# One more output row reads the last frequency pair in place, and two table quarters are transposed earlier

## The chip, the cores and the metric

The kernel runs on one core of one Trainium2 chip. The metric is the device time of one execution in microseconds; the time given for a kernel is the median of its runs. A profile is of one execution, and its own time is named beside it.

## What is computed

A long-convolution block with a token-mixing MLP behind it, on 2048 tokens of 448 channels:

```python
def _A_ref(q, k, v, shift_k, ssm_k, ssm_D):
    k_shift = sum of 4 shifted copies of k, each times a column of shift_k
    kv = k_shift * v
    y = irfft(rfft(kv padded to 4096) * rfft(ssm_k padded to 4096))[:2048]
    y = y + kv * ssm_D
    return q * y
def _B_ref(x, w1, b1, w2, b2):
    h = _layernorm(x)                       # over the channels
    u = gelu(einsum("bsd,sf->bdf", h, w1) + b1)
    return transposed(einsum("bdf,fs->bds", u, w2) + b2)
x = A_q
h = x + _A_ref(_layernorm(x), A_k, A_v, A_shift_k, A_ssm_k, A_ssm_D)
h2 = h + _B_ref(_layernorm(h), B_w1, B_b1, B_w2, B_b2)
```

S is 2048, D is 448, F is 1792; inputs and output are bfloat16.

## The kernel before

**Tiling.** A token index is split as 16 q + r: 128 partitions q and R = 16 rows r. All of SBUF is one tensor, `arena`, all of PSUM one tensor, `ps` (eight banks), so the profile names only these two; its line numbers tell the steps apart. The steps have tags, which are also the names in the order lists.

**Stages.** The transform of length 4096 is done as matmuls in two steps each way. `kT` and `kv` transpose the filter and form kv. `k1` and `u1` (`emit_stage1`, L1059) are the first forward step for the filter and for kv; the result goes by DMA from one layout to the next (L1075). `k2` and `u2` (`emit_stage2`, L1094) are the second forward step, in place in TK and TU; the evictions are those of `evac` (L738 and L739 on ScalarE, L741 and L742 on VectorE). `i1` (`emit_products_i1`) works by eight pairs: two products on VectorE (L1160), 16 matmuls (L1177), two evictions (halves h = 0 and 1) back into TU, and then DMAs that carry the pair from TU to TZ, where a partition holds one frequency (L1200, L1189). The pairs run in the order 0, 6, 3, 4, 5, 2, 1, 7: i1.1, i1.14, i1.8, i1.10, i1.12, i1.6, i1.4 and i1.16 are the names of their matmul steps, so i1.4 is pair 1 and i1.16 is pair 7, the last. `i2` (`emit_i2`) is the second inverse step, row by row: two matmuls (L1299) of ET, the transposed sine table, with TZ.

**In-place rows.** For rows r < NZ, here rows 0 and 1, TZ holds zeros in the place of the last pair, and four more matmuls (L1307) add that pair from TU directly, with EW as the table. EW is filled by POOL (zeros, L1134) and by small DMAs of parts of ET (L1127). These rows need not wait for the last pair's DMA; rows from NZ on do. The four stand behind the two TZ matmuls of their row.

**Behind i2.** A gate (L1316 on ScalarE, L1318 on VectorE; rows 0 to 3 have none, their normalised input XN comes from `xn`, L1269), a combination with the input on VectorE (L1326, L1337), then the second and third layernorm: rows 0 and 1 one at a time (L1343, L1346, L1375), the others by groups of two with a square on ScalarE (L1355), small steps on POOL (L1365 to L1375) and a power on POOL (L1379). A normalised row Q is written by VectorE (L1385). `mlp` accumulates over the rows: mlp.r is seven matmuls with Q row r (L1432); then come the other half of the first layer (L1442) and the second layer (L1453, with the last addition at L1456).

**Sine table.** `ct` makes ET from E by 8 transposes (L1108) and one eviction a quarter. Quarter 0 (step ct0.0) is made within i1, quarters 1 to 3 (steps ct.0, ct.1, ct.2) behind pair 7's matmuls, among warm-up matmuls (`warm`, L1210) that keep PE at work while it waits.

**Order.** A planner in the kernel puts every operation on an engine and finds the semaphores, but each engine's sequence is written out in `ORDER`, in one list each for pe, act, dve, pool and sp. An engine works its list strictly in order; a token such as `i1.16:18` is operation 18 of that step. The parts around the change are:

```python
"pe":  ... u1.15:0-7 k2.2:0-3 ... i1.16:1-7 i1.16:10-16 ... ct.2:0-7 warm.12:0 warm.3:0 ct.0:0-7 ct.1:0-6 warm.2:0 i2.1:0-1 i2.2:0-3 ...
"act": ... i1.4:8 i1.4:17 xn.1:0 xn.2:0 i1.16:18 i1.16:9 ct.2:8 ct.0:8 xn.5:0 xn.4:0 ct.1:8 i2.29:0 ...
"dve": ... u1.11:8 k2.3:4 k2.7:4 bias.1:0 k2.11:4 k2.15:5 u2.1:5 ... i1.9:0 ct0.0:8 q.1:0 ...
"sp":  ... ct0.1:5 ct0.1:2-4 i1.1:20 ... i1.4:20 i1.16:22 i1.16:20 i1.16:19 w1a.1:0 ...
```

`bias.1` is the cast of b2 (L939). `q` holds the statistics of the input rows (VectorE L1236, L1238; POOL L1244, L1247). The W1 loads from w1a.1 on wait for the four DMAs of pair 7.

## Time and profile before

| | us |
|---|---|
| median of the three runs | 173.62 |
| lowest and highest run | 172.66, 175.37 |
| the profiled execution | 172.93 |
| its span | 171.0 |

| engine | busy us | share of the span |
|---|---|---|
| PE (matmul) | 162.0 | 95% |
| PEld (weight load) | 95.1 | 56% |
| DVE (VectorE) | 98.9 | 58% |
| ACT (ScalarE) | 92.9 | 54% |
| POOL (GpSimd) | 60.3 | 35% |

In the profile, times are in microseconds from the start of the span. A timeline row gives start, length, engine, line, operation, what is written and read, the count, and in brackets the idle time ahead of it with what ended it. A row of the chain gives start, length and what the chain stood on. Instructions of one engine overlap a little at their ends, so a row's length is somewhat more than the time to the next start. The granted clock of PE is 1.00 in the whole span.

### The profile page before, as it was taken

The numbers are of one execution on the slowest core, as the hardware profiler recorded it, in microseconds if no ns is written. First come the engines' busy times: TensorE is split into PE (matmuls) and PEld (weight loads), VectorE is DVE, ScalarE is ACT, GpSimd is POOL, SyncE is SP. The second block draws the span as 40 slices with busy tenths as digits, with TensorE's granted clock in tenths as the row PEclk, the third lists the DMA queues.
The fourth block names the chain that finished last, engine by engine and source line by source line (L and its number), as shares of the span: only waits on it lengthen the run. The fifth ranks groups of instructions, "written<-read, shape, count | busy, mean of one in ns | idle before, by whom it ended". The sixth has DMA issues, their size and how long they took to land.

```text
span 171.0 us, 3568 instructions
## 1 busy us (share of the span) xinstructions
PE 162.0 (95%) x1425; PEld 95.1 (56%) x1425; DVE 98.9 (58%) x187; ACT 92.9 (54%) x133; POOL 60.3 (35%) x154
## 2 busy tenths in 40 slices
PE   6989999988889999999999999999999999999993
PEld 2766745442334443464455555555567777777783
DVE  7988988869699999999968810000003223132232
ACT  3698787998889999999887437321210000000000
POOL 8346627591810496576888820000000000000000
PEclk9999999999999999999999999999999999999999
DMA  5999677675859667665999999970000111101111
GB/s 167 406 310 384 192 246 274 246 281 210 270 147 372 236 182 217 186 185 183 319 361 404 413 419 421 418 324 13 0 0 4 54 54 54 54 0 58 54 54 54
DMA packets 15740, 35.15 MB, mean 206 GB/s; under 512 B 3628, under 2 KB 9980, under 8 KB 15724
## 3 DMA queue, kind: packets, MB, share of 16 engines
q1 hardware_dynamic: 12924, 29.08, 47.2%
q0 software_dynamic: 2656, 5.76, 10.5%
q8 instruction: 11, 0.18, 0.4%
q10 hardware_dynamic: 144, 0.08, 0.2%
q14 instruction: 5, 0.04, 0.1%
HBM read 22.05 MB, written 1.84 MB: 140 GB/s over the span
## 4 chain that ended last, share of the span: by engine, by line
PE 66%; ACT 14%; DMA 12%; DVE 3%; issue 2%; SPq 2%; POOL 0%; DVEq 0%
PE ps L1453 25%; PE ps L1442 12%; PE ps L1432 11%; ACT arena L738 7%; DMA arena<-arena 7%; DMA arena<-in_A_ssm_k_dram 5%; PE ps L1094 5%; ACT arena L1069 4%; PE ps L1177 4%; PE ps L1059 2%; PE ps L1299 2%; ACT arena L1316 2%; PE ps L992 1%; DVE arena L742 1%; PE ps L1307 1%
## 5 line engine op out<-in xcount | busy, mean ns | idle before, releaser
L1456 DVE SCALAR_TENSOR_TENSOR arena<-ps,arena 128x448 bf16<-128x448 f32 (+2 forms) x17 | 11.2, 656 | 57.4 <-PE ps L1453 57.3
L1453 PE MATMUL ps<-arena 128*128 128x448 bf16 (+2 forms) x238 | 42.7, 342 | 0.0
L1453 PEld LDWEIGHTS ps<-arena 128*128 128x128 bf16 x238 | 33.3, 145 | 9.5
L738 ACT CAST arena<-ps 128x896 bf16<-128x896 f32 x30 | 24.6, 1021 | 0.5 <-PE ps L1094 0.5
L1432 PE MATMUL ps<-arena 128*128 128x448 bf16 x112 | 22.5, 353 | 0.0
L1069 ACT CAST arena<-ps 128x896 bf16<-128x896 f32 x24 | 20.5, 915 | 3.7 <-PE ps L1059 3.7
L1075 POOL DMA_DIRECT2D arena<-arena x32 | 17.6, 553 | 12.7 <-ACT arena L1069 11.1
L1442 PE MATMUL ps<-arena 128*128 128x448 bf16 x112 | 21.3, 352 | 0.0
L1422 ACT ACTIVATE arena<-ps,arena 128x448 bf16<-128x448 f32 x14 | 8.2, 639 | 18.7 <-PE ps L1442 14.6
L1094 PE MATMUL ps<-arena 128*64 128x448 bf16 x128 | 15.2, 359 | 2.9 <-ACT arena L1069 0.9
L1160 DVE TENSOR_TENSOR arena<-arena 128x1792 bf16<-128x1792 bf16 x16 | 16.7, 1086 | 0.3 <-ACT arena L738 0.3
L1432 PEld LDWEIGHTS ps<-arena 128*128 128x128 bf16 x112 | 10.8, 98 | 10.6 <-DVE arena L1385 0.9
L1442 PEld LDWEIGHTS ps<-arena 128*128 128x128 bf16 x112 | 11.0, 98 | 10.2
L1059 PE MATMUL ps<-arena 128*32 128x448 bf16 x256 | 15.0, 355 | 0.8 <-DVE arena L1007 0.5
L1177 PE MATMUL ps<-arena 64*128 64x448 bf16 x128 | 14.5, 351 | 0.1
L1200 POOL DMA_DIRECT2D arena<-arena x15 | 8.7, 583 | 13.8 <-ACT arena L738 13.8
L1094 PEld LDWEIGHTS ps<-arena 128*64 128x64 f16 x128 | 6.2, 108 | 10.8 <-ACT arena L738 3.0
L1177 PEld LDWEIGHTS ps<-arena 64*128 64x128 f16 x128 | 6.1, 94 | 8.2 <-ACT arena L738 2.5
L1007 DVE TENSOR_TENSOR arena<-ps,arena 128x512 bf16<-128x512 f32 (+1 forms) x16 | 9.1, 618 | 2.1 <-PE ps L992 1.8
L1355 ACT ACTIVATE arena<-arena 128x448 bf16<-128x448 bf16 x14 | 8.0, 572 | 3.7 <-DVE arena L1326 3.6
L738 ACT COPY arena<-ps 128x1024 bf16<-128x1024 bf16 (+1 forms) x8 | 8.1, 1073 | 3.3 <-PE ps L966 3.3
L1059 PEld LDWEIGHTS ps<-arena 128*32 128x32 f16 x256 | 5.1, 95 | 7.6 <-DVE arena L1007 2.5
(97 smaller groups left out, 194.4 us busy)
## 6 DMA issues: line engine op xcount, KB each, us to landing
arena<-in_B_w_dram SPq DMA_DIRECT2D x8, 896.0 KB, 9.5
arena<-in_B_w_dram SPq DMA_DIRECT2D x2, 2048.0 KB, 17.8
arena<-arena POOLq DMA_DIRECT2D x32, 112.0 KB, 3.1
arena<-arena SPq DMA_DIRECT2D x16, 224.0 KB, 3.3
arena<-in_B_w_dram SPq DMA_DIRECT2D x2, 1536.0 KB, 20.3
arena<-in_A_k_dram SPq DMA_DIRECT2D x4, 448.0 KB, 6.0
arena<-in_A_v_dram SPq DMA_DIRECT2D x4, 448.0 KB, 9.0
arena<-in_A_q_dram SPq DMA_DIRECT2D x4, 448.0 KB, 5.5
```

The costliest lines, as they stand in the source:

```text
L738: return e.copy(out=dst(), in_=src())
L1007: return e.tensor_tensor(out=v, in0=u.rearrange("p t (r d) -> p t r d", d=64), in1=v, op=ALU.mult)
L1059: op("pe", lambda e, W, b=b, r=r, q=q, x=x, c0=c0: e.matmul(PS[32 * q:32 * q + 32, b.slots[x], 0:D], E[:, 2 * r + x, c0:c0 + 32], src[:, r ...
L1069: return e.copy(out=dst, in_=Ppair(b)) if W == "act" else e.tensor_copy(out=dst, in_=Ppair(b))
L1075: shuf[tag].append(op(q_, lambda e, W, g=g, i=i, a=a, nu=nu, jh=jh: e.dma_start(T[a + i:a + i + 4 * nu - 3:4].rearrange("p (j k) c d -> p ...
L1094: op("pe", lambda e, W, b=bs[h], h=h, j=j, c=c, par=par: e.matmul(PS[64 * par:64 * par + 64, b.slots[c], 0:D], FW[:, 64 * c:64 * c + 64], ...
L1160: op("dve", lambda e, W, m=m, i=i: e.tensor_tensor(out=MR(m.slots[0]).rearrange("p (x y) d -> p x y d", x=2), in0=TU[:, i].unsqueeze(2).br ...
L1177: k = op("pe", lambda e, W, b=bs[h], m=ms[h], par=par, t=t, tab=tab, xy=xy, P=P: e.matmul(Pb(b, par), tab[P, :], MR(m.slots[0])[P, xy, :], ...
L1432: op("pe", lambda e, W, r=r, fc=fc, b=bs[fc]: e.matmul(Pb(b), W1A[:, r, 128 * fc:128 * fc + 128], Q[:, r, :], start=(r == 0), stop=(r == R ...
L1442: op("pe", lambda e, W, r=r, fc=fc, b=b: e.matmul(Pb(b), W1B[:, r, 128 * (fc - n0):128 * (fc - n0) + 128], Q[:, r, :], start=(r == 0), sto ...
L1453: op("pe", lambda e, W, r=r, fc=fc, b=b, d0=d0, d1=d1: e.matmul(Pb(b)[:, d0:d1], W2[fc // 7][:, fc % 7, r:S:R], G[:, fc, d0:d1], start=(fc ...
L1456: op("dve", lambda e, W, r=r, b=b, d0=d0, d1=d1: e.scalar_tensor_tensor(out=X[:, r, d0:d1], in0=Pb(b)[:, d0:d1], scalar=bm[:, r:r + 1], in ...
```

## The change

Five things are changed, and all five lists are written anew.

1. NZ is 3 in place of 2: row 2 is in place too. EW has 12 tables in place of 8 (its clearing on POOL grows by half), SP has six EW copies in place of four, and pair 7's DMAs carry 13 rows in place of 14.
2. In `emit_i2` the four in-place matmuls of a row are the first of their accumulation, half 1 ahead of half 0; the two TZ matmuls follow.
3. Pair 7's DMA of half 0, first of the two, goes from SP to POOL, so that each queue has two.
4. The planner's rule that the late quarters of the sine table follow i1 is gone. In the lists quarters 1 and 2 now stand behind u1.15, ahead of the last part of k2, and VectorE evicts them; quarter 3 stays on ScalarE.
5. For rows 2 and 3 the mean and variance are three small VectorE steps in place of four on POOL (1 + EPS is folded into the square's scale); the power stays on POOL.

```diff
-"pe":  u1.11:0-7 u1.14:0-7 u1.15:0-7 k2.2:0-3 k2.3:0-3 k2.7:0-3
+"pe":  u1.11:0-7 u1.14:0-7 u1.15:0-7 ct.0:0-7 ct.1:0-7 k2.2:0-3 k2.3:0-3 warm.3:0 k2.7:0-3
...
+"pe":  i1.16:10-15 i1.16:1 i1.16:16-17 i1.16:2-8 warm.0:0 warm.8:0 i2.17:0-1 i2.1:0 i2.9:0-2 i2.1:1-3 i2.9:3 i2.17:2-3
+       i2.18:0-1 i2.10:0 i2.2:0-1 warm.7:0 i2.10:1 i2.46:0-1 i2.21:0 i2.29:0-1 i2.33:0 i2.21:1 i2.55:0-1 i2.33:1 i2.42:0-1
+       i2.59:0-1 mlp.0:3-4 mlp.0:0-1 mlp.0:6 mlp.0:5 mlp.1:6 mlp.1:5 mlp.1:0 mlp.1:3 mlp.1:1 i2.68:0-1 mlp.0:2 mlp.1:2 mlp.1:4
+       mlp.2:1-3
...
+"act": u2.3:4-5 u2.15:4-5 i1.6:18 i1.6:9 i1.4:17 i1.4:8 xn.5:0 i1.16:18 i1.16:9 xn.2:0 xn.4:0 xn.1:0 ct.2:8 i2.20:0 i2.47:0
...
+"dve": kv.8:12 bias.1:0 kv.10:24-25
...
+"dve": u1.10:8 u1.11:8 ct.0:8 ct.1:8 k2.3:4 k2.7:4 k2.11:5 k2.15:4 u2.1:5 i1.0:0 i1.1:0 i1.14:0 i1.13:0 q.1:2 q.1:0 q.1:3
+       i1.8:0 q.1:1 i1.7:0 i1.9:0 i1.10:0 xn.0:1 ct0.0:8
...
+"dve": q.8:2 i2.19:0 i2.3:0 i2.11:0 i2.4:0 i2.12:0 i2.5:0 i2.13:0 i2.6:0 q.8:3 i2.14:0 i2.22:0 i2.8:0 i2.24:1 i2.24:0 q.7:2
+       i2.25:0 q.7:3 i2.16:0 q.8:0 i2.31:0 q.8:1 i2.35:0 i2.27:0
...
+"pool": ew.0:0 ew.0:2 ew.0:1 q.1:4-5 i1.14:19 i1.14:21 i1.8:19 i1.8:21 i1.14:20 i1.10:19 i1.8:20 q.2:4-5 i1.1:19 i1.8:22 xn.0:0
+        i1.12:19 xn.3:0 ew.0:3 i1.14:22 i1.6:19-20 i1.4:18 i1.6:22 i1.16:21 i1.16:19
...
+"sp":  ct0.1:5 ct0.1:2-4 ct0.1:7 ct0.1:6 i1.1:20 i1.1:22 i1.10:21 i1.1:21 i1.12:21 i1.6:21 i1.4:20 i1.16:22 i1.16:20 w1a.1:0
...
-        NZ = 2
+        NZ = 3
...
-                       r=[...], bw=[b], kind="tr", safter=i1_last[-1:])
+                       r=[...], bw=[b], kind="tr")
...
-                            k = op("pool" if h and par == 0 else "sp", ...
+                            k = op("pool" if par == 0 else "sp", ...
...
-                    for h in range(2):
-                        k = op("pe", ... e.matmul(Pb(b), ET[:, 2 * r + h, :], TZ[:, r, h, :], start=(h == 0), stop=(h == 1 and r >= NZ)),
...
                     if r < NZ:
...
-                        for h in range(2):
+                        for h in (1, 0):
                             for jx in range(2):
                                 j = R - 2 + jx
-                                k = op("pe", ... e.matmul(Pb(b), EW[:, 4 * r + 2 * jx + h, :], TU[:, j, h, :], start=False, stop=(h == 1 and jx == 1)),
+                                k = op("pe", ... e.matmul(Pb(b), EW[:, 4 * r + 2 * jx + h, :], TU[:, j, h, :], start=(h == 1 and jx == 0), stop=False),
...
+                    for h in range(2):
+                        k = op("pe", ... e.matmul(Pb(b), ET[:, 2 * r + h, :], TZ[:, r, h, :], start=(h == 0 and r >= NZ), stop=(h == 1)),
...
+                if g == 2:
+                    op("dve", ... e.scalar_tensor_tensor(out=hs[:, 6:8], in0=hs[:, 0:2], scalar=-(1.0 + EPS) / (D * D), in1=hs[:, 0:2], ...
+                    op("dve", ... e.tensor_scalar(out=hs[:, 4:6], in0=hs[:, 0:2], scalar1=1.0 / D, ...
...
+                if g == 2:
+                    op("dve", ... e.scalar_tensor_tensor(out=hs[:, 8:10], in0=hs[:, 6:8], scalar=EPS * EPS, in1=hs[:, 2:4], ...
```

In the new names row 0 is i2.1 (in place) and i2.2 (TZ), row 1 i2.9 and i2.10, row 2 i2.17 and i2.18; rows 3, 4, 5, 6, 7, 8, 9 and 10 are i2.21, 29, 33, 42, 46, 55, 59 and 68. Row 0 is combined by i2.3, row 1 by i2.11, row 2 by i2.19, row 3 by i2.22; Q rows 0, 1, 2 are i2.8, i2.16, i2.27. i2.24 and i2.25 are the three small steps of rows 2 and 3.

More of the change, by code (lines that the diff above doesn't have):

```diff
@@ L1297, in emit_i2 @@
                     tz = [(o_TZ + r * 2 * DB, 2 * DB)]
-                    for h in range(2):
-                        k = op("pe", lambda e, W, b=b, r=r, h=h: e.matmul(
-                            Pb(b), ET[:, 2 * r + h, :], TZ[:, r, h, :], start=(h == 0), stop=(h == 1 and r >= NZ)),
-                           r=[r_ET(r)] + tz, bw=[b], n=D, after=av[-1:] if r >= 8 and h == 0 else ())
                     if r < NZ:
-                        sch.t0 += 0.2
-                        for h in range(2):
+                        k = None
+                        for h in (1, 0):
                             for jx in range(2):
```

36 lines of the change are left out of this document (26 added, 10 removed), and 95 rows, old and new, of the table ORDER.

## The prediction

> **What bounds the kernel now.** I read the chain of waits first, then the stretches by engine, then the timeline of each engine around the hand-over from the transform to the last matmuls. The chain gives the place:
>
> ```profile
> 70.01 1.14 ACT arena L738
> 71.15 0.28 issue
> 71.43 3.76 DMA arena<-arena
> 75.19 0.09 issue
> 75.28 0.54 PE ps L1299 x2
> ```
> ```profile
> 75.28:84.12 8.84, 8.74 (x45) 4.08 (x46) 8.80 (x31) 8.65 (x18) 6.13 (x13) 1.00 0.71 224
> 84.12:168.00 83.88, 83.88 (x455) 54.41 (x455) 22.07 (x52) 18.83 (x40) 12.95 (x32) 1.00 0.43 167
> ```
>
> These are two stretches, with the busy time and count of PE, PEld, DVE, ACT and POOL, then clock, DMA share and GB/s. From 84.12 us PE is busy for 83.88 of 83.88 us at full clock, and from there on the change leaves it the same matmuls. So the time is decided by when PE reaches the state that it has at 84.12: i2 rows 0 to 10 done, mlp.0 and mlp.1 done, mlp.2 next. Ahead of that the chain stands on a PSUM eviction of ScalarE, then on a transfer of TZ.
>
> ```profile
> 48.36 22.77 ACT L738 CAST arena<-ps 128x896 bf16<-128x896 f32 x28 [0.51 <-PE ps L1094]
> 70.81 1.57 ACT L1269 ACTIVATE arena<-arena 128x448 f32<-128x448 bf16 x2
> 72.12 1.87 ACT L738 CAST arena<-ps 128x896 bf16<-128x896 f32 x2
> ```
>
> ScalarE runs 28 evictions without a gap, starting one each 0.8 us ((70.81 - 48.36)/28). The last two of the 28 are pair 1 (i1.4); two normalised rows follow (0.66 us apart: 72.12 - 70.81 over two), and then the last pair's evictions (i1.16).
>
> ```profile
> 75.28 0.54 PE L1299 MATMUL ps<-arena 128*128 128x448 bf16 x2 [0.36 <-DMA arena<-arena]
> 75.65 0.92 PE L1307 MATMUL ps<-arena 128*128 128x448 bf16 x4
> ...
> 77.60 2.81 PE L1299 MATMUL ps<-arena 128*128 128x448 bf16 x14
> 80.42 1.31 PE L1432 MATMUL ps<-arena 128*128 128x448 bf16 x6
> ...
> 84.12 1.50 PE L1432 MATMUL ps<-arena 128*128 128x448 bf16 x7
> ```
>
> One 448-column matmul starts 0.19 us after the one before ((75.65 - 75.28)/2). Rows 0 and 1 with their eight in-place matmuls, which stand behind TZ, take PE from 75.28 to 77.60.
>
> The profiled execution took 172.93 us (span 171.0); the median of the three runs is 173.62, 0.69 above. I work against 172.93 and add 0.69 at the end.
>
> **Part by part: in-place rows and their order.** In the new ScalarE list the same 28 evictions stand ahead of pair 1's end, and one normalised row in place of two ahead of i1.16: the last pair's evictions end at 73.3 instead of 74.0 (72.12 + 1.87 less 0.66). The two halves are evicted 0.8 us apart, half 1 first, so its six matmuls can start at 72.6, the other six behind them: 12 x 0.19 = 2.3 us, done at 74.9. That lies under the wait for TZ, which warm-up matmuls fill today. When TZ lands only six matmuls remain for rows 0 to 2, with one warm-up matmul: 7 x 0.19 = 1.3, so they end at 76.6, where today three rows end at 77.98 (77.60 + 2 x 0.19). PE gains 1.4 us here, although row 2 adds four matmuls. Two transfers (rows 3 to 15) now come from POOL and two from SP:
>
> ```profile
> 58.32 2.68 SPq L1127 DMA_DIRECT2D arena<-arena  x4
> ...
> 73.20 2.19 SPq L1189 DMA_DIRECT2D arena<-arena  x3
> 77.48 0.38 SPq L1405 DMA_DIRECT2D arena<-in_B_w_dram  x1
> ```
> ```profile
> arena<-arena POOLq DMA_DIRECT2D x1, 98.0 KB, 2.8
> ```
>
> Today SP issues three in a row, 0.73 us each, and the W1 load that waits for all four goes at 77.48. With two each, 0.7 us earlier, and 2.8 us to landing, POOL's second goes at about 73.6 and lands near 76.4: row 3 is not late.
>
> **Where that gain meets the next queue.** mlp.0 needs Q row 0, mlp.2 needs Q row 2, and both come from VectorE:
>
> ```profile
> 75.50 1.14 DVE L1236 BATCH_NORM_STATS2 arena<-arena 128x6 f32<-128x448 bf16 x2
> 76.61 0.68 DVE L1337 SCALAR_TENSOR_TENSOR arena<-ps,arena 128x448 bf16<-128x448 f32 x1
> ...
> 79.98 0.39 DVE L1385 TENSOR_SCALAR arena<-arena 128x448 bf16<-128x448 bf16 x1
> ...
> 81.19 0.68 DVE L1326 SCALAR_TENSOR_TENSOR arena<-arena 128x448 bf16<-128x448 bf16 x1
> ...
> 81.79 0.68 DVE L1326 SCALAR_TENSOR_TENSOR arena<-arena 128x448 bf16<-128x448 bf16 x1
> ...
> 83.66 0.41 DVE L1385 TENSOR_SCALAR arena<-arena 128x448 bf16<-128x448 bf16 x1
> ```
> ```profile
> 79.33 0.55 POOL L1379 TENSOR_TENSOR arena<-arena 128x1 f32<-128x1 f32 x1 [0.50 <-DVE arena L1375]
> ...
> 81.06 0.31 POOL L1365 TENSOR_SCALAR arena<-arena 128x2 f32<-128x2 f32 x1 [0.28 <-DVE arena L1337]
> 81.45 0.47 POOL L1368 TENSOR_TENSOR arena<-arena 128x2 f32<-128x2 f32 x1
> ...
> 82.89 0.73 POOL L1379 TENSOR_TENSOR arena<-arena 128x2 f32<-128x2 f32 x1
> ...
> 84.02 0.19 POOL L1368 TENSOR_TENSOR arena<-arena 128x2 f32<-128x2 f32 x1
> ```
>
> A combined row keeps VectorE 0.6 us (81.19 to 81.79), a statistics pass 0.55 (75.50 to 76.61 for two), a normalised row 0.3 to 0.4, a small one about 0.1 by my estimate (its recorded 0.15 us or so overlaps the next). With TZ landing as today, row 2's matmuls end at 75.85 (75.28 + 0.19 + 0.35 of pipeline). Behind that the new list has three combined rows (1.8), two statistics passes (1.1) and three small ones (0.3): 79.05. POOL's power takes 0.55 plus some 0.1 of hand-over: 79.7; row 3's combined row hides it; Q row 0 takes until 80.15, and mlp.0 starts near 80.2 instead of 80.42. PE has run out of i2 rows by then (76.6 + 14 x 0.19 = 79.3), so 0.9 us of its 1.4 are given back as idle time.
>
> To Q row 2, from 80.1: two small, one statistics, two small, normalised row 1 (0.2 + 0.55 + 0.2 + 0.35) makes 81.4; statistics, combined, small, combined, normalised row 2 (0.55 + 0.6 + 0.1 + 0.6 + 0.35) makes 83.6. mlp.2 starts at 83.65 instead of 84.12: **0.47 us**. The statistics of rows 2 and 3 that move from POOL to VectorE take 1.8 us from 81.06 to the power at 82.89 today; as three small VectorE instructions they put that power at 81.1 to 81.9, under VectorE's own work, so the power stops being what ends last there and VectorE's queue is. PE's part (six mlp.0, eight others, row 10) would be ready at 83.4; it is not what counts.
>
> **The two quarters of the sine table**, and what else moves on VectorE:
>
> ```profile
> 43.16 1.70 PE L1094 MATMUL ps<-arena 128*64 128x448 bf16 x16 [0.94 <-ACT arena L1069]
> ...
> 44.11 2.09 DVE L742 TENSOR_SCALAR arena<-ps 128x896 bf16<-128x896 f32 x2 [1.54 <-PE ps L1094]
> ...
> 46.11 1.57 DVE L939 CAST arena<-arena 128x16 f32<-128x16 bf16 x1
> ...
> 46.71 0.94 POOL L1134 MEMSET arena<- 128x1024 f16 x1
> ```
> ```profile
> 73.72 1.00 PE L1108 MATMUL ps<-arena 128*128 128x128 f16 x15
> ```
> ```profile
> 57.60 0.69 DVE L741 COPY arena<-ps 128x1024 f16<-128x1024 f16 x1
> 58.21 1.14 DVE L1236 BATCH_NORM_STATS2 arena<-arena 128x6 f32<-128x448 bf16 x2
> ```
>
> Sixteen transposes are about 1.0 us of PE, put where it idles 0.94 us ahead of 43.16; their two copies are 2 x 0.6 us (57.60 to 58.21) in VectorE's idle 1.54 us ahead of 44.11. If that cover is gone, all that follows starts up to 1.2 us later. I charge 0.1. On ScalarE two evictions leave the stretch behind i1.16, where the gates of i2 then start earlier. The cast of b2, which ends at 47.68, 0.03 us after POOL's memset, holds back the VectorE eviction behind it, which follows within 0.1 us and by itself takes 1.09 (two, 1.0 apart, take 2.09): it could have ended near 47.3, and PE waits for it. Moved to an earlier stage, the cast gives back at most 0.37. The Trainium skill's page "SBUF — State Buffer" (section "SBUF: two separate sides") says that a GpSimd operation and such a VectorE operation take a port pair by turns, the loser blocked until the other ends; by that rule the 0.37 is all regained if POOL is idle where the cast now stands. The trace agrees: the 16-element cast lasts 1.57 us, as long as POOL's operations do.
>
> **What moves in the DMA queues.** SP issues six small EW copies where it issues four (0.67 each), and they wait for a VectorE copy that the new list puts behind three more statistics instructions (about 1.4 us): 2.7 us later for the five TZ transfers queued behind them. Pair 2's evictions come two slots later on ScalarE (1.6 us), and so do its transfers on POOL.
>
> ```profile
> arena<-arena POOLq DMA_DIRECT2D x1, 196.0 KB, 5.0
> ```
>
> That row is pair 2's today, issued at 68.19, 5.0 us to landing; the last one (pair 1, 71.43) takes 3.76. Nothing shows how they share when pair 2's goes at 69.8. Bounds: nothing lost, since pair 1's issue does not move (an earlier landing by 0.4 at best, as the stage ahead starts earlier); at worst pair 2's lands at 74.8 and pair 1's 1.8 to 2.0 behind it, at 76.8, 1.6 late. I take 0.35 late, nearer to the first, because the transfers' bytes are the same and the issue is not later.
>
> **Sum:** 0.47, plus 0.27 (0.37 - 0.1) for the earlier start, less 0.35: 0.4 us gained. 172.93 - 0.4 = 172.5; on the scale of the medians 173.2.
>
> **The rivals.** *PE's whole gain stays.* VectorE's queue was counted from rows that overlap; if its list runs ahead, or rows 0 to 2 are finished in another order, PE keeps the 1.4 us and the 0.27: 171.3, as a median 172.0. For it: ScalarE has two evictions less to do ahead of the gates. Against it: VectorE is busy for 8.80 of the 8.84 us of this stretch today.
>
> *Slower: TZ lands late.* The place is pair 1's transfer behind pair 2's on POOL's queue; the price is what it lands later than 75.19, less the 0.47. It decides from 75.66 on. At 76.8 it costs 1.6 - 0.47 = 1.1: 174.0, as a median 174.7. For it: the 5.0 us above, and five SP transfers pushed into the same stretch. Against it: the two transfers issued last are no later.
>
> *The moved statistics collide with POOL's power.* They run near 80.2, when POOL's power for row 1 does (0.55 to 0.73 us). If VectorE is held until it ends, up to 0.5 us go and nothing is left: 172.9, as a median 173.6. By the same page and section of the Trainium skill this is what would happen, since whoever starts first keeps the port pair. The rows show rather POOL held: its L1368 takes 0.47 us beside a combined row and 0.19 otherwise, while L1326 takes 0.68 each time.
>
> *The in-place matmuls are not early.* If the last pair's evictions stay at 74.0, four of the twelve fall behind the landing: the row 2 start slips 0.4, no gain, 173.5.
>
> **How the numbers follow.** Forecast 0.46; whole gain 0.20; late TZ 0.21; collision 0.08; not early 0.05. On the medians: 173.2, 172.0, 174.7, 173.6, 173.5. The three runs of before lie 2.7 us apart, so a median is uncertain by some 0.5; the range reaches from below the whole gain, 171.6, to above the late TZ, 175.2, and leaves out less than 2 in 10. Two per cent, about what a measurement of this kernel can tell from no change, is 3.5 us: no case reaches it by its own price. A late TZ joined by lost cover in the sine-table step (1.2) comes nearest, so slower 0.08, faster 0.04, within 0.88.
>
> **What would show it.** In the profile after: twelve in-place matmuls ahead of the landing, done by 75; the start of the ScalarE run near 48.1; the landing that starts the TZ matmuls between 75 and 76; PE idle for about 0.9 us just ahead of mlp.0, near 80.2; mlp.2 at 83.5 to 83.9, with VectorE's normalised row as the releaser. I am wrong if PE does not idle there, if the landing lies past 76, or if the wait ahead of mlp.2 ends on POOL.

## The result, and the profile after

The changed kernel takes **179.36 us**, the median of six runs (177.69 to 180.58); the kernel before takes 173.83 beside it. The ratio is **1.0336, 95% interval 1.0252 to 1.0419**: slower, where 173.2 and "within 2%" were forecast.

Of the six runs the three with a granted clock of 1.00 took 177.69, 178.75 and 179.10. The profiled execution took 180.58 us (span 178.8), the longest of the six: its granted clock is 0.50 from 13.50 to 16.90 us, and ScalarE's run of evictions starts at 51.03 us where before has 48.36. Profiles of other kernels with the same lists up to there start it at 47.89 to 49.35. So the traces are compared below from that start on, where the clock is 1.00 in both. The profile of one experiment (best1) has the same half clock near 14 us and is read in the same way; of another (a_ord2, granted clock 0.76) only the times are read.

The page of after, the shares of the chain that ended last, by engine:

```profile
PE 64%; DMA 10%; DVE 9%; POOL 7%; issue 4%; ACT 3%; SPq 1%; DVEq 0%; POOLq 0%; ACTq 0%
```

and the same line of before:

```profile
PE 66%; ACT 14%; DMA 12%; DVE 3%; issue 2%; SPq 2%; POOL 0%; DVEq 0%
```

ScalarE's evictions have left the chain; POOL, which was no part of it, and VectorE have come in. To see where, the time is cut at five events that both kernels have: ScalarE's eviction u2.1:4 starts (the first of the 28), POOL issues pair 1's transfer (i1.4:18), it lands, mlp.2 starts, mlp.17 starts. From mlp.17 to the end both take 66.4 us. The stretches by engine, of before and then of after (from-to; length; busy time and count of PE, PEld, DVE, ACT, POOL; clock, DMA share, GB/s):

```profile
48.36:71.43 23.07, 22.13 (x195) 9.35 (x193) 22.74 (x31) 23.07 (x29) 9.60 (x16) 1.00 0.74 235
71.43:75.19 3.76, 3.48 (x38) 2.16 (x33) 3.66 (x12) 3.76 (x6) 3.00 (x7) 1.00 0.57 158
75.19:84.12 8.93, 8.75 (x45) 4.12 (x46) 8.89 (x31) 8.74 (x18) 6.22 (x13) 1.00 0.71 224
84.12:104.56 20.44, 20.44 (x109) 10.54 (x109) 11.82 (x37) 11.36 (x28) 12.95 (x32) 1.00 1.03 395
```
```profile
51.03:76.88 25.85, 24.42 (x211) 10.01 (x210) 24.00 (x37) 24.43 (x31) 15.36 (x20) 1.00 0.65 204
76.88:81.97 5.09, 3.07 (x16) 1.20 (x14) 3.36 (x11) 4.23 (x6) 4.68 (x9) 1.00 0.70 195
81.97:90.25 8.28, 7.81 (x38) 3.06 (x38) 7.61 (x28) 6.12 (x13) 2.25 (x5) 1.00 0.73 226
90.25:112.33 22.08, 20.92 (x110) 10.24 (x110) 12.35 (x37) 10.76 (x27) 13.19 (x33) 1.00 1.03 396
```

I call the four stretches A (evictions), B (transfer), C (landing to mlp.2) and D (mlp.2 to mlp.17). They went from 23.07, 3.76, 8.93 and 20.44 to 25.85, 5.09, 8.28 and 22.08: **+2.78, +1.33, -0.65 and +1.64, together 5.1 us**. C is the stretch that the prediction worked out. The loss lies in the three others. Of D's 22.08 us PE is busy for 20.92, where before it is busy all through. In A, POOL is busy for 15.36 us instead of 9.60 with only four instructions more.

The chain of waits of after, in parts, from 67.86 us to the first TZ matmul:

```profile
67.86 0.98 POOL arena L1247
...
70.30 0.33 POOL arena L1203
...
71.52 1.05 POOL arena L1259
72.58 0.56 POOL arena L1203
...
73.16 0.94 POOL arena L1259
74.11 0.22 POOL arena L1143
...
75.19 1.12 POOL arena L1203 x2
...
78.02 4.02 DMA arena<-arena
...
82.06 0.55 PE ps L1312 x2
```

L1203 and L1192 are the transfers of pairs. Between them, on the same queue, stand small POOL steps on 128x2 or 128x72 elements: statistics (L1247, L1250), two input scales (L1259), a copy for EW (L1143). ScalarE ends pair 1's second eviction at 75.49 (it starts at 74.59); its transfer, behind three others that were held up, is issued at 76.88, 1.39 us later (before: 71.14 to 71.43, 0.29). It lands at 81.97, 0.09 us ahead of the first TZ matmul; the chain's DMA row starts from a later issue, one of the last pair's, which rows 0 to 2 do not take from TZ. So A's 2.78 are 1.1 of waiting on POOL's queue and 1.7 by which the run of evictions itself is longer.

### The profile page after: what moved, and what is told of

Read it like the earlier page. It is cut to its first block, busy times and chain, and to the rows that moved or that the text cites. A ratio compares the mean times of both kernels' runs of the same rounds, so it can differ in the third digit from the quotient of the medians.

```text
span 178.8 us, 3582 instructions
## 1 busy us (share of the span) xinstructions
PE 166.5 (93%) x1429; PEld 95.5 (53%) x1429; DVE 100.2 (56%) x192; ACT 92.3 (52%) x131; POOL 64.3 (36%) x151
## 4 chain that ended last, share of the span: by engine, by line
PE 64%; DMA 10%; DVE 9%; POOL 7%; issue 4%; ACT 3%; SPq 1%; DVEq 0%; POOLq 0%; ACTq 0%
PE ps L1471 24%; PE ps L1460 12%; PE ps L1450 7%; PE ps L1097 5%; DMA arena<-in_A_ssm_k_dram 5%; PE ps L1062 5%; DMA arena<-arena 5%; PE ps L995 3%; PE ps L1180 3%; POOL arena L1203 2%; DVE arena L1163 2%; ACT arena L742 2%; PE ps L969 2%; PE ps L1213 1%; POOL arena L1259 1%
## 5 line engine op out<-in xcount | busy, mean ns | idle before, releaser
L741 ACT CAST arena<-ps 128x896 bf16<-128x896 f32 x30 | 25.1, 930 | 1.4 <-PE ps L1180 0.8
L1072 ACT CAST arena<-ps 128x896 bf16<-128x896 f32 x24 | 20.6, 913 | 5.8 <-PE ps L1062 5.7
L1078 POOL DMA_DIRECT2D arena<-arena x32 | 17.6, 553 | 14.6 <-ACT arena L1072 12.9
L1450 PE MATMUL ps<-arena 128*128 128x448 bf16 x112 | 22.5, 353 | 0.1
L1460 PE MATMUL ps<-arena 128*128 128x448 bf16 x112 | 21.3, 352 | 0.0
L1062 PE MATMUL ps<-arena 128*32 128x448 bf16 x256 | 15.6, 368 | 0.8 <-DVE arena L1010 0.5
L1312 PE MATMUL ps<-arena 128*128 128x448 bf16 x32 | 7.8, 354 | 3.6 <-DMA arena<-arena 2.1
L744 DVE COPY arena<-ps 128x1024 bf16<-128x1024 bf16 (+2 forms) x14 | 8.9, 649 | 2.8 <-PE ps L1041 2.0
L1180 PEld LDWEIGHTS ps<-arena 64*128 64x128 f16 x128 | 5.6, 94 | 8.9 <-DVE arena L1163 2.5
L1239 DVE BATCH_NORM_STATS2 arena<-arena 128x6 f32<-128x448 bf16 x16 | 9.5, 610 | 1.2 <-DMA arena<-in_A_q_dram 1.2
```

Source lines behind the costliest of these rows:

```text
L741: return e.copy(out=dst(), in_=src())
L1062: op("pe", lambda e, W, b=b, r=r, q=q, x=x, c0=c0: e.matmul(PS[32 * q:32 * q + 32, b.slots[x], 0:D], E[:, 2 * r + x, c0:c0 + 32], src[:, r ...
L1072: return e.copy(out=dst, in_=Ppair(b)) if W == "act" else e.tensor_copy(out=dst, in_=Ppair(b))
L1078: shuf[tag].append(op(q_, lambda e, W, g=g, i=i, a=a, nu=nu, jh=jh: e.dma_start(T[a + i:a + i + 4 * nu - 3:4].rearrange("p (j k) c d -> p ...
L1180: k = op("pe", lambda e, W, b=bs[h], m=ms[h], par=par, t=t, tab=tab, xy=xy, P=P: e.matmul(Pb(b, par), tab[P, :], MR(m.slots[0])[P, xy, :], ...
L1239: op("dve", lambda e, W, bs=bs, r=r: e.bn_stats(out=bs, in_=X[:, r, :]), r=[(o_X + r * DB, DB)], w=[(ob, 24)], n=D, kind="1x")
```

## The experiments

Each edit changes order lists of the five queues, or is the kernel before with a part of the change; none leaves out work that the result needs. In their traces the same code stands 2 to 21 lines above the numbers of after. Ratios are to the kernel before on the same chip. The table has every kernel that was run, with the four stretches of its profiled execution:

| kernel | A | B | C | D | sum | ratio [95%] |
|---|---|---|---|---|---|---|
| before | 23.07 | 3.76 | 8.93 | 20.44 | 56.20 | |
| after | 25.85 | 5.09 | 8.28 | 22.08 | 61.30 | 1.0336 [1.0252, 1.0419] |
| a_pool | 24.99 | 5.24 | 8.36 | 22.09 | 60.68 | 1.0230 [1.0169, 1.0291] |
| a_stat | 26.34 | 5.00 | 8.27 | 22.09 | 61.70 | 1.0332 [1.0274, 1.0390] |
| a_sp | 25.75 | 4.57 | 8.28 | 22.09 | 60.69 | 1.0204 [1.0122, 1.0286] |
| a_all | 25.17 | 4.47 | 8.50 | 22.10 | 60.24 | 1.0213 [1.0159, 1.0268] |
| a_warm | 25.06 | 4.01 | 9.39 | 22.09 | 60.55 | 1.0253 [1.0211, 1.0295] |
| b_warm | 23.90 | 3.76 | 8.94 | 20.56 | 57.16 | 1.0050 [1.0026, 1.0073] |
| b_place | 23.07 | 4.13 | 9.62 | 20.44 | 57.26 | 1.0071 [1.0044, 1.0098] |
| b_ct | 23.07 | 3.71 | 8.95 | 20.44 | 56.17 | 0.9992 [0.9957, 1.0026] |
| a_ord | 23.07 | 3.77 | 13.71 | 21.86 | 62.41 | 1.0341 [1.0304, 1.0378] |
| a_ord_q8 | 23.07 | 4.35 | 13.73 | 22.64 | 63.79 | 1.0431 [1.0401, 1.0462] |
| b_both | 23.07 | 3.77 | 9.17 | 20.44 | 56.45 | 1.0031 [1.0008, 1.0054] |
| b_stat | 23.07 | 4.38 | 8.80 | 20.44 | 56.69 | 1.0035 [1.0012, 1.0058] |
| a_ord2 | | | | | | 1.0161 [1.0091, 1.0230] |
| b_u2 | 24.04 | 4.27 | 8.72 | 20.44 | 57.46 | 1.0082 [1.0051, 1.0112] |
| best1 | 23.07 | 4.47 | 8.17 | 20.43 | 56.14 | 0.9988 [0.9956, 1.0021] |
| best2 | 23.07 | 4.15 | 8.47 | 20.43 | 56.11 | 0.9990 [0.9946, 1.0034] |
| a_mix | 23.07 | 4.30 | 12.34 | 20.43 | 60.14 | 1.0290 [1.0205, 1.0374] |
| b_q | 23.07 | 4.03 | 9.02 | 20.44 | 56.55 | 1.0030 [0.9997, 1.0062] |

The stretches are of one execution each. A repeats: it is 23.07 in every kernel with the old order up to there. B does not: b_both and b_stat have the same lists up to the landing and differ by 0.6, and so do a_ord and a_ord_q8. So a difference of that size in B is not read from one pair of kernels.

### Small steps ahead of transfers

Theory: small steps that the new lists put ahead of pair transfers hold these up. a_pool takes xn.0, xn.3 and the EW copy off the transfers' way, a_stat puts the first statistics behind ct0.0 again, a_sp puts SP's EW copies behind five pair transfers, a_all does all three.

```diff
 pool (a_pool)
-i1.8:22 xn.0:0 i1.12:19 xn.3:0 ew.0:3 i1.14:22
+i1.8:22 i1.12:19 i1.14:22 ... i1.16:21 i1.16:19 xn.0:0 xn.3:0
 dve (a_stat)
-i1.13:0 q.1:2 q.1:0 q.1:3 i1.8:0 q.1:1 i1.7:0 i1.9:0 i1.10:0 xn.0:1 ct0.0:8
+i1.13:0 i1.8:0 i1.7:0 i1.9:0 i1.10:0 ct0.0:8 q.1:2 q.1:0 q.1:3 q.1:1
 sp (a_sp)
-ct0.1:5 ct0.1:2-4 ct0.1:7 ct0.1:6 i1.1:20 i1.1:22 i1.10:21 i1.1:21 i1.12:21
+i1.1:20 i1.1:22 i1.10:21 i1.1:21 i1.12:21 ct0.1:5 ct0.1:2-4 ct0.1:7 ct0.1:6
```

> The changed kernel with the small POOL steps xn.0, xn.3 and ew.0:3 taken out from between the pair transfers (ew.0:3 to the head, the two others behind the last pair's transfers; ScalarE's xn.5 then follows i1.16's evictions). In the changed kernel's profile these three last 0.95 to 1.17 us each, pair 1's evictions end at 75.49 and its POOL transfer is issued at 76.88. Theory POOL (the small steps ahead of the transfers make TZ late): the issue follows the evictions within 0.4 us, TZ lands 1.4 to 2.4 us earlier, the time falls from 179.4 to 177.0 to 178.0. Theory STATISTICS (the early input statistics hold up VectorE and with it everything) and theory SP (the EW copies ahead of SP's transfers): the landing stays where another queue sets it, 178.8 to 179.6.

> The changed kernel with the statistics of rows 0 and 1 (q.1) behind ct0.0:8 on VectorE and behind i1.14:20 on POOL, as before, and xn.0:1 behind i1.3. Theory STATISTICS: VectorE no longer idles 1.16 us for the load of the input rows nor 0.62 us for POOL, POOL's first pair transfer goes 1.6 us earlier, and the time falls by 1.5 to 2 us, to 177.4 to 177.9. Theory POOL: the transfers still stand behind the small steps, at most 0.7 us gained, 178.7 or more. Theory SP: ct0.0:8 comes about 3 us earlier and with it the EW copies, so it gains as well, up to 2 us; it is told apart by the run that moves the copies alone.

> The changed kernel with SP's six EW copies behind its five pair transfers of pairs 0, 4, 5, in place of ahead of them. Theory SP: those five go about 4 us earlier, TZ lands 1 to 2 us earlier, 177.4 to 178.4. Theories POOL and STATISTICS: the last transfer to land is POOL's, which is issued late, and the time stays within 0.6 us of 179.4.

> The three edits together. If the three causes are all that is wrong behind the early part: evictions of pair 1 as early against the start of the evictions as before, TZ landing within 0.7 us of before against the same start, PE's 0.65 us gain between landing and mlp.2, and still some 1.6 us idle in PE between mlp.2 and the second half of the first layer: 174 to 175.5. If a cause is missing (the early table quarters, the longer EW clearing, the first 15 us): 176.5 or more.

Measured: 1.0230, 1.0332, 1.0204 and 1.0213, against 1.0336. Taking the steps off POOL's way shortens A by 0.86 us (25.85 to 24.99), but A and B together by 0.7 only, where a_pool's theory had the landing 1.4 to 2.4 earlier. With the copies off SP's way B is 4.01 to 4.57 (a_sp, a_all, a_warm), otherwise 5.00 to 5.24 (after, a_pool, a_stat). a_stat alone does nothing for the time. By the stretches all three together regain 1.1 of the 5.1 us; by the medians 1.2%, 2.1 us, with intervals that overlap. Either way more than half of the loss stands with POOL's queue free: in a_all pair 1's transfer is issued 0.3 us behind its eviction, as before, and A is still 25.17. So it came out as the case of a_all's expectation in which a cause is missing.

### The warm-up matmuls

In a_all VectorE waits twice for PE in the i1 stage (start, length, ..., idle before and releaser):

```profile
53.98 4.10 DVE L1160 TENSOR_TENSOR arena<-arena 128x1792 bf16<-128x1792 bf16 x4 [0.60 <-PE ps L1177]
58.96 0.69 DVE L741 COPY arena<-ps 128x1024 f16<-128x1024 f16 x1 [0.89 <-PE ps L1108]
```

The new PE list has ten of the fourteen warm-up matmuls ahead of pair 2's matmuls (i1.6); the old one has none there, its first stands behind them. a_warm takes them out of a_all; b_warm puts them into the kernel before.

```diff
 pe (a_warm, on a_all)
-u2.13:3 warm.10:0 warm.6:0 u2.9:0-3 u2.8:0-3 warm.13:0 warm.12:0 u2.7:0 warm.1:0 ...
+u2.13:3 u2.9:0-3 u2.8:0-3 u2.7:0 ... i1.16:2-8 warm.10:0 warm.6:0 warm.13:0 warm.12:0 ...
 pe (b_warm, on before)
+u2.13:0-3 warm.10:0 warm.6:0 ... i1.14:8 warm.5:0 warm.9:0 i1.8:1-7 ...
```

> The kernel with all three moves (176.67 us), and besides the ten warm-up matmuls that the new list put into the u2 and i1 stages stand behind the last pair's matmuls again. Theory: ten matmuls of 0.2 us, seven of them ahead of the products of i1.8 and i1.10, make PE late as the supplier of VectorE and ScalarE: VectorE waits 0.61 us ahead of the product of i1.8 and 0.89 us ahead of the copy ct0.0 in the trace with all three moves, ScalarE 1.07 us ahead of i1.12. Without them the first i1 matmul starts near 51.4 instead of 52.4, pair 1's last eviction starts at 70.6 to 70.9 instead of 71.9, and the time is 175.4 to 175.8. Rival: the half-by-half order of the i1 matmuls and the swapped steps are what makes PE late, or VectorE's wait for POOL's statistics (0.62 us ahead of xn.3) takes the place of the others: 176.3 to 176.8.

> The kernel before, with the ten warm-up matmuls at the places of the new list and nothing else. Theory: PE becomes late in the u2 and i1 stages by up to 7 x 0.2 = 1.4 us, of which PE's idle time there today (0.2 to 0.4 us ahead of u2.8, u2.7) hides 0.4 to 0.6: pair 1's end and the time 0.8 to 1.2 us later, 173.7 to 174.1. Rival: PE has that room, ScalarE's 0.8 us pace sets the stage: 172.9 within 0.3.

b_warm came as the theory said: A 0.83 us longer, ratio 1.0050. a_warm did not: A only 0.11 shorter, the time no better. Two reasons stand in its trace. VectorE's copy ct0.0 still waits for PE, now 1.20 us:

```profile
58.80 0.69 DVE L742 COPY arena<-ps 128x1024 f16<-128x1024 f16 x1 [1.20 <-PE ps L1109]
```

and the twelve warm-up matmuls behind the last pair (L1211, from 73.59) push the in-place matmuls (L1304) past the landing at 76.98, so the TZ matmuls (L1310) start at 78.14:

```profile
73.59 2.44 PE L1211 MATMUL ps<-arena 128*128 128x448 f16 x12
75.87 2.43 PE L1304 MATMUL ps<-arena 128*128 128x448 bf16 x12
78.14 1.11 PE L1310 MATMUL ps<-arena 128*128 128x448 bf16 x5
```

So warm-ups in the stage cost, but with the new order something else ahead of ct0.0 costs the same time beside them: the two do not simply add. That is the next suspect: u2.10 and u2.11 stand ahead of i1.8 and ct0.0.

### The two parts, each alone and together

b_place is the kernel before with the in-place part alone, b_ct with the quarters and the cast alone, b_both with both, all else in the old order; b_stat adds the statistics of rows 2 and 3 on VectorE.

```diff
 pe (b_both)
-u1.15:0-7 k2.2:0-3
+u1.15:0-7 ct.0:0-7 ct.1:0-7 k2.2:0-3
-warm.3:0 ct.0:0-7 ct.1:0-6 warm.2:0 i2.1:0-1 i2.2:0-3 i2.9:0 ct.1:7 i2.9:1 i2.10:0-3
+warm.3:0 i2.1:0-3 i2.9:0-3 i2.17:0-3 warm.2:0 i2.2:0-1 i2.10:0-1
 pool (b_both)
-i2.23:0-2 i2.24:0 i2.25:0
+i2.24:0-2 i2.25:0 i2.26:0
 dve (b_stat, on b_both; the four POOL steps i2.24 and i2.25 go)
+i2.22:0 i2.24:1 i2.24:0 i2.16:0 i2.31:0 i2.25:0 i2.35:0
```

> The kernel before, with the in-place rows alone: three rows, their matmuls first, the odd half's transfer of the last pair on POOL, six EW copies; every other instruction in its old place, the table where it was, the statistics on POOL. By the prediction's own steps (0.47 us gained by mlp.2, up to 0.35 back through later transfers): 172.4 to 172.8. Rival: the idea itself costs, because SP issues two more EW copies (1.4 us) ahead of its five pair transfers and the landing ahead of the first TZ matmul comes later than 75.3: 173.5 to 174.5.

> The kernel before, with the second part alone: two quarters of the sine table transposed and copied behind the last forward stage, and the cast of b2 at its new, earlier place. By the prediction's steps: ScalarE's run starts near 48.1 instead of 48.36, the quarters hide; with the two evictions off ScalarE 172.4 to 172.7. Rival: the cover is gone and the u2 stage starts up to 1.2 us later: 173.5 to 174.1.

> The kernel before with both named parts (in-place rows first with three rows, and the two early table quarters with the cast), every other instruction in its old order, statistics of rows 2 and 3 on POOL. With the in-place rows alone (173.87 beside 172.46) the twelve matmuls stood behind the table's transposes and started only at 74.4, so that the first TZ matmul came 1.5 us behind the landing. Theory: with the quarters gone from there they start near 73 and are done at the landing, which is at 74.5 to 75.3; mlp.2 comes 8.4 to 8.8 behind it: 171.6 to 172.6, faster than before or the same. Rival: the last pair's fourth piece on POOL (landed at 77.3 in the run with the in-place rows alone, 1.0 behind the third) or VectorE's list holds mlp.0 as there: 173.0 to 173.9.

> As b_both, and the statistics of rows 2 and 3 are three small VectorE instructions, as in the change. Theory: POOL is spared four instructions ahead of the power of rows 2 and 3, the normalised row 2 comes earlier, mlp.2 0.2 to 0.5 us earlier than in b_both. Rival: VectorE's list sets mlp.2, and three more instructions on it make it 0.3 us later than b_both.

None is faster than before. The quarters with the cast cost nothing and gain nothing that the time shows (0.9992). In b_place the in-place matmuls stand behind the table's transposes and start at 74.36; with both parts they start at 73.62. This is PE's timeline in b_both (L1300 in-place, L1306 TZ, L1431 mlp):

```profile
73.62 2.43 PE L1300 MATMUL ps<-arena 128*128 128x448 bf16 x12
...
76.08 0.92 PE L1306 MATMUL ps<-arena 128*128 128x448 bf16 x4
77.27 2.82 PE L1306 MATMUL ps<-arena 128*128 128x448 bf16 x14 [0.28 <-DMA arena<-arena]
80.56 1.31 PE L1431 MATMUL ps<-arena 128*128 128x448 bf16 x6 [0.47 <-DVE arena L1384]
```

The landing is at 75.09. PE is 1.0 us late for it, then waits for the last pair's fourth piece, and then, as forecast, for VectorE's normalised row 0. mlp.0 starts at 80.56 where before has 80.42 (its row stands in the prediction), although PE had four fewer matmuls to make behind the landing for each of rows 0 and 1. VectorE, for which the trace shows no idle time from 75.61 to that row, takes the whole gain. Both times lie where the rivals had them; in b_both the rival's reason, VectorE's list, is what the trace shows, in b_place it is the transposes ahead. Moving the statistics changes nothing that the time shows (1.0035 beside 1.0031).

### The order of the i1 stage and the lists of the last stage

a_ord has the old lists of all queues to the end of i1, with both parts, and from there those of after; a_ord_q8 besides moves POOL's q.8 ahead of the power of rows 4 and 5.

```diff
 pool (a_ord_q8, on a_ord)
-i2.26:0 i2.37:0-2 i2.38:0 i2.39:0 q.8:4 i2.50:0 q.8:5
+i2.26:0 q.8:4-5 i2.37:0-2 i2.38:0 i2.39:0 i2.50:0
```

> The changed kernel whose lists of all five queues are, up to the end of the i1 stage (the last pair's evictions and transfers), in the order of the kernel before, with the two table quarters and the cast of b2 early; behind that its own lists. Theory: the new order of the u2 and i1 stages is most of the loss: u2.10 and u2.11 ahead of i1.8 make the transposes ct0.0 1.2 us late, VectorE waits for them with ten instructions behind, ScalarE then waits 1.07 us for i1.12. Without it pair 1's transfer is issued near 70.8 and lands at 74.5 to 75.3, mlp.2 comes 8.4 behind that, mlp.17 21.9 behind mlp.2: span 171.2 to 172.0, time 172.9 to 173.7. Rival: the loss sits in the in-place rows themselves (two pieces of the last pair on POOL, three banks of PSUM held by rows begun early): 175 or more.

> As a_ord, and POOL makes the statistics of the last input rows (q.8, two instructions) ahead of the power of rows 4 and 5 again, as before, where the new list has them behind three or four instructions of that group. Theory: those two finish 4.7 us behind mlp.2 in the trace with all three moves (before: 3.8), ScalarE's gate of row 12 waits for them with 0.53 us idle, that gate frees the PSUM bank of row 13, and PE idles 0.97 us ahead of row 13: 0.9 to 1.2 us earlier than a_ord. Rival: the wait only passes to the normalised rows 4 and 5, now behind a later power: no more than 0.3 us from a_ord.

Both failed, and a_ord answers only half of its question. A and B are back at 23.07 and 3.77, but the joint of the two halves made a wait that neither kernel has. This is VectorE in a_ord:

```profile
74.79 0.16 DVE L1258 SCALAR_TENSOR_TENSOR arena<-arena 128x2 f32<-128x2 f32 x1 [4.88 <-POOL arena L1246]
```

A 0.16 us step (xn.3) waits 4.88 us for a POOL step that the old list has behind the transfers, with sixteen statistics instructions queued behind it; C is 13.71. PE then idles for 4.32 us ahead of 82.20, and its granted clock is half from 81.70 to 85.10:

```profile
81.70:85.10 3.40, 2.90 (x8) 1.09 (x9) 3.40 (x15) 2.77 (x6) 1.43 (x3) 0.50 1.03 351
```

The same shows in C of a_ord_q8 and a_mix, and every run of these three has a mean granted clock of 0.98 to 0.99, so their times hold that besides the waits. For A the answer stands: with the old order up to there it is 23.07. In a_ord_q8 POOL's q.8 waits in turn, 3.1 us, for statistics (q.7) that VectorE's list has late, and holds the power behind it. a_ord2 joins the halves behind xn.3 instead; b_u2 puts one swap of the new i1 order into b_both.

```diff
 pe (b_u2, on b_both)
-i1.8:1-7 i1.8:10-16 i1.8:8 i1.8:17 ct0.0:0-7 u2.10:0-3 u2.11:0-3
+u2.10:0-3 u2.11:0-3 i1.8:1-7 i1.8:10-16 i1.8:8 i1.8:17 ct0.0:0-7
 act (b_u2)
-i1.8:9 i1.8:18 u2.11:4-5
+u2.11:4-5 i1.8:9 i1.8:18
 dve (a_ord2, on a_ord)
-i1.16:0 xn.3:1 q.3:1 q.4:0 q.5:0 ...
+i1.16:0 q.4:0 q.4:2-3 q.4:1 q.3:1-3 q.5:0 q.5:2-3 q.5:1 q.6:2 q.6:0-1 xn.3:1 ...
```

> The kernel with both parts in the old order (173.2) up to the end of the i1 stage with VectorE's statistics and POOL's xn.3 behind it, and from there on the lists of the changed kernel. Theory: the i1 stage is then as in b_both (pair 1 lands near 75.1) and only the new lists of the last stage are left: landing to mlp.2 8.2 to 8.6 us, mlp.2 to mlp.17 21.9 us where the old lists take 20.44: 1.2 to 1.6 us above b_both, 174.4 to 174.8. Rival: the old front takes the cause of those waits away too (POOL free earlier): within 0.4 us of b_both.

> The kernel with both parts in the old order, and u2.10 and u2.11 with their evictions ahead of i1.8 and of the transposes ct0.0, as in the change; nothing else. Theory: the copy ct0.0 on VectorE starts 0.8 to 1.2 us later, and with it the product of i1.11, ScalarE's evictions of i1.12 and pair 1's end: 0.6 to 1.2 us above b_both, 173.8 to 174.4. Rival: ScalarE's 0.8 us pace has room for it, since the same 28 evictions are to be made: within 0.3 us of b_both.

b_u2's time is as its theory had it. a_ord2 is at 1.0161: with the front of b_both, the last stage's lists cost 1.3% over b_both's 1.0031, 2.2 us; the 1.2 to 1.6 us expected lie within its interval. b_u2 is at 1.0082, A 0.97 us longer than in b_both. VectorE in b_u2, with the copy ct0.0 (the row of b_both has none of this idle time, at 57.47):

```profile
58.12 0.69 DVE L738 COPY arena<-ps 128x1024 f16<-128x1024 f16 x1 [1.48 <-PE ps L1105]
```

Added up, b_u2 and b_warm, 0.97 and 0.83, come to most of the 2.10 us by which A is longer in a_all. Each was measured in the old order; that they add in the new one is not shown, and a_warm speaks against it.

### Which list of the last stage

a_mix takes PE's and ScalarE's lists of a_ord2 with VectorE's and POOL's of b_stat. b_q puts the suspected places of q.7 and q.8 into b_stat.

```diff
 dve (b_q, on b_stat)
-xn.3:1 q.7:0 q.7:2 ... q.7:1 q.7:3 q.8:0 q.8:2 i2.27:0 ...
+xn.3:1 q.7:2 ... q.7:3 q.8:0 q.8:2 i2.27:0 q.7:0 q.8:1 q.8:3 i2.28:0 i2.44:0 q.7:1 ...
 pool (b_q)
-q.8:4-5 i2.50:0-2
+q.8:4 i2.50:0 q.8:5 i2.50:1-2
```

> The old order up to the end of the i1 stage, behind it PE's and ScalarE's lists of the changed kernel, but VectorE's and POOL's in the order of b_stat. Theory: the loss of the last stage is VectorE's and POOL's order, above all statistics q.7 and q.8 that come late, so with the old one only b_stat's time is left: 172.9 to 173.5 (ratio up to 1.006). Rival: PE's list, which begins rows in another order and mixes mlp.4 to mlp.6, or ScalarE's order of gates costs the 1.3%: 174.8 or more.

> As b_stat, with the two passes q.7:0 and q.7:1 on VectorE behind rows 2 and 4 and q.8's second POOL step behind the first of rows 4 and 5, as in the change, and nothing else. Theory: POOL's two steps of q.8 and the power of rows 4 and 5 come about 1 us later, ScalarE's gate of row 12 waits for them, that gate frees row 13's PSUM bank, PE idles there: 0.6 to 1.5 us above b_stat, 173.7 to 174.6. Rival: the old lists have slack there: within 0.3 us of b_stat.

b_q has no loss (D 20.44): those entries alone are not it. a_mix splits the answer. The stretch from mlp.2 to mlp.17 in a_mix:

```profile
87.70:108.13 20.43, 20.43 (x109) 10.57 (x108) 11.03 (x34) 9.95 (x25) 12.20 (x29) 1.00 1.04 412
```

PE has no idle time in it, with its own changed list. So that list by itself does not cost D's 1.64 us, which points to VectorE's and POOL's. It is not proof: C is 12.34, 3.4 us more than before, and gave these two queues time to get ahead (POOL's last statistics, q.8, end 2.4 us behind mlp.2 here, 3.2 in b_stat, 4.9 in after). C is so long because ScalarE's list has the square of row 2 ahead of the gates and the old VectorE list makes row 2 late (PE, then ScalarE, of a_mix):

```profile
81.52 2.30 PE L1307 MATMUL ps<-arena 128*128 128x448 bf16 x7 [2.86 <-ACT arena L1316]
```
```profile
80.19 0.58 ACT L1355 ACTIVATE arena<-arena 128x448 bf16<-128x448 bf16 x1 [2.26 <-DVE arena L1337]
```

The lists of one stage fit each other: a_mix, half of one set with half of another, is at 1.0290, where a_ord2 is at 1.0161 and b_stat at 1.0035.

### Is the idea worth something with its own order?

best1 is b_stat with three warm-up matmuls fewer, the in-place matmuls directly behind the table's transposes, q.7:2 behind the first combined rows, and the normalised rows 2 and 3 ahead of the last statistics; best2 also gives the odd half's transfer back to SP.

```diff
 pe (best1, on b_stat)
-warm.12:0 warm.3:0 i2.1:0-3 i2.9:0-3 i2.17:0-3 warm.2:0
+i2.1:0-1 i2.9:0-1 i2.17:0-1 i2.1:2-3 i2.9:2-3 i2.17:2-3
 dve (best1)
-xn.3:1 q.7:0 q.7:2 i2.3:0 ... i2.35:0 q.7:1 q.7:3 q.8:0 q.8:2 i2.27:0 q.8:1 q.8:3 i2.28:0
+xn.3:1 q.7:0 i2.3:0 ... i2.25:0 q.7:2 i2.35:0 i2.27:0 i2.28:0 q.8:0 q.8:2 q.7:1 q.7:3 q.8:1 q.8:3
```

> As b_stat, with three warm-up matmuls fewer, the in-place matmuls of half 1 of all three rows first and behind the table's transposes at once, one statistics pass of VectorE (q.7) behind the first combined rows instead of ahead of them, and VectorE's normalised rows 2 and 3 ahead of the last four statistics passes. Theory: PE is done with the in-place rows at the landing, VectorE reaches row 0 0.5 us earlier, mlp.0 comes 0.3 and mlp.2 0.4 to 0.9 us earlier than in b_stat: 172.2 to 172.8. Rival: row 3 waits for the last pair's fourth piece (77.2) as before, and mlp.0 stays where it is: 173.0 or more.

> As best1, with the odd half's transfer of the last pair on the SP queue again (three on SP, one on POOL, as before). Theory: the fourth piece no longer lands behind the others on POOL's queue, row 3 does not wait (0.6 us idle on PE in b_stat): up to 0.4 us better than best1, 172.0 to 172.6. Rival: on SP it is issued third and lands no earlier: the same as best1.

172.37 and 172.13 beside 172.44: 0.9988 and 0.9990, some 0.45% below b_stat, with intervals that overlap, and the same as before. C is 8.17 and 8.47, 0.8 and 0.5 us shorter than before's, but B is 4.47 and 4.15 instead of 3.76, and takes nearly all of it back. best2 is no better than best1, as its rival had it. In the table the ten kernels that have the in-place rows but not the new order of the i1 stage have a B of 3.77 to 4.47, the three without these rows (before, b_warm, b_ct) 3.71 to 3.76; which of the moved transfers does that was not tested. No version was found that is faster than the kernel before.

## Why the prediction was wrong, point by point

**The in-place matmuls are early: in after, but only because the landing is late.** PE in after, in-place (L1306) and then TZ (L1312):

```profile
77.50 2.44 PE L1306 MATMUL ps<-arena 128*128 128x448 bf16 x12
82.06 1.11 PE L1312 MATMUL ps<-arena 128*128 128x448 bf16 x5 [2.12 <-DMA arena<-arena]
```

They are done 2.0 us before the landing, at 79.9 instead of 74.9. Where the landing is as early as forecast (b_both, 75.09) they end at 76.05, 1.0 us behind it. So the rival that had them late is not out; what hid it in after was luck.

**Landing to mlp.2 0.47 us shorter: near in size (0.65), half right in the path.** I had VectorE's full queue decide and PE idle 0.9 us ahead of mlp.0. mlp.2 does wait for VectorE's normalised row 2 (it ends at 90.19, mlp.2 starts at 90.25). But PE idles only 0.1 us ahead of mlp.0, and VectorE's list is empty at the landing, because that is late:

```profile
82.64 0.68 DVE L1342 SCALAR_TENSOR_TENSOR arena<-ps,arena 128x448 bf16<-128x448 f32 x1 [2.29 <-PE ps L1312]
```

It waits 2.29 us for row 0. Where the landing is early (b_both), VectorE still has statistics to do, mlp.0 is not earlier at all, and C is 9.17, longer than before's. So that 0.65 comes near 0.47 is luck as well: the term was counted behind a landing at 75.2 that the change does not have.

**The quarters and the cast: no loss, as forecast; the gain of 0.27 is not shown.** ScalarE's run starts at 47.68 in b_ct (48.36 before; 48.1 was forecast). But it starts at 47.92 in b_warm and 48.10 in b_place, which have the quarters and the cast in their old places, and at 48.26 in b_both, which has them early.

**The step that failed** is the sentence "in the new ScalarE list the same 28 evictions stand ahead of pair 1's end", with the pace of 0.8 us kept, and the bound beside it, "nothing lost, since pair 1's issue does not move". The count is right and the pace is not kept. ScalarE in after:

```profile
52.21 11.54 ACT L741 CAST arena<-ps 128x896 bf16<-128x896 f32 x14 [0.27 <-PE ps L1097]
64.17 11.32 ACT L741 CAST arena<-ps 128x896 bf16<-128x896 f32 x13 [0.42 <-PE ps L1180]
```

Behind the first one at 51.03, 14 in 11.96 us (64.17 - 52.21) and 13 in 11.32 make 0.85 and 0.87 us each instead of 0.8. Where nothing holds ScalarE it still starts one each 0.80 us (nine from 56.36 to 62.73); the waits in between end on PE, as the brackets show. PE is late as the supplier: it has warm-up matmuls among its work (0.83 us of A in b_warm) and makes u2.10 and u2.11 ahead of i1.8 and ct0.0 (0.97 in b_u2). The diff showed both, and I read only the names of the steps that the change is about. The issue then moved by another 1.10 us, through steps which I had priced at nothing: the small POOL steps now ahead of the transfers. This is what they take in before and in after, with VectorE's products beside those of after:

```profile
61.38 1.66 POOL L1247 TENSOR_TENSOR arena<-arena 128x2 f32<-128x2 f32 x1
...
66.52 0.21 POOL L1256 TENSOR_TENSOR arena<-arena 128x2 f32<-128x2 f32 x1
...
74.13 0.74 POOL L1247 TENSOR_TENSOR arena<-arena 128x2 f32<-128x2 f32 x1
```
```profile
67.86 0.97 POOL L1247 TENSOR_SCALAR arena<-arena 128x2 f32<-128x2 f32 x1 [0.54 <-DVE arena L1241]
71.52 1.05 POOL L1259 TENSOR_TENSOR arena<-arena 128x2 f32<-128x2 f32 x1
73.16 0.94 POOL L1259 TENSOR_TENSOR arena<-arena 128x2 f32<-128x2 f32 x1
74.05 1.17 POOL L1143 COPY arena<-arena 128x72 f16<-128x72 f16 x1
```
```profile
70.44 2.08 DVE L1163 TENSOR_TENSOR arena<-arena 128x1792 bf16<-128x1792 bf16 x2
72.98 1.07 DVE L1163 TENSOR_TENSOR arena<-arena 128x1792 bf16<-128x1792 bf16 x1
74.07 1.06 DVE L1163 TENSOR_TENSOR arena<-arena 128x1792 bf16<-128x1792 bf16 x1
```

The two scales (L1256 before, L1259 after) took 0.2 us and take 1.0. They end at 72.57, 74.10 and, the copy, at 75.22, each 0.05 to 0.09 us behind the end of a product of VectorE (72.52, 74.05, 75.13). The Trainium skill's page "SBUF — State Buffer" (section "SBUF: two separate sides") has this rule: a VectorE operation with two inputs from SBUF and a GpSimd operation that reads SBUF hold a shared port pair by turns, each for its whole length. The trace agrees. Before's own trace had the size: L1247 takes 1.66 us at 61.38 with a product beside it (the product of i1.12 starts at 61.38), and 0.74 at 74.13 with none. The prediction cited that rule for the cast of b2 and for POOL's power, and did not apply it to the POOL steps that the diff moves.

**TZ late: the right rival, too small.** The place was right (pair 1's transfer behind the others on POOL's queue). The price was a landing 1.6 us later, 1.1 after the 0.47, all of it in B. B is 1.33 longer; A, which it took as unchanged, adds 2.78. The landing, at 81.97, is past 76, which the prediction gave as a sign of being wrong.

**From mlp.2 on "the same matmuls": wrong by 1.64 us.** The matmuls are the same and PE waits among them. PE, and ScalarE's gate that frees the PSUM bank for row 13, in after:

```profile
95.93 0.55 PE L1312 MATMUL ps<-arena 128*128 128x448 bf16 x2 [0.97 <-ACT arena L1321]
```
```profile
95.15 0.72 ACT L1321 ACTIVATE arena<-ps,arena 128x448 f32<-128x448 f32 x1 [0.54 <-POOL arena L1250]
```

The gate waits for POOL's last statistics, which end at 95.11. That PE was busy all through this stretch before said that its suppliers were in time with the old lists, not that they had room. a_mix points to VectorE's and POOL's lists; b_q shows that the places of q.7 and q.8 alone, put into the old lists, do not do it. Which entries it is stays open.

**The collision of the moved statistics with POOL's power: no cost**, nor gain, in b_stat against b_both.

The account of the 5.1 us is then: 1.1 on POOL's queue and 1.7 in evictions that wait for PE in A, 1.3 in B, 1.6 in D, less 0.65 in C. Not assigned are some 0.3 us of A in a_all beyond b_u2 and b_warm. The medians of after and a_all (179.36, 176.67) lie 2.7 us apart where the stretches show 1.1. Of that, 1.0 is in the kernel before, which took 173.83 beside the one and 172.88 beside the other. After's 178.75, the middle one of the three runs named with the result, is 4.9 above its before, and a_all's 176.67 is 3.8 above its own: 1.1 apart, as in the stretches. The two named parts by themselves are within 0.3% of before.
